# A fused attention and two-MLP kernel: weight conversion moved to the end of the first attention, and a second product in place of a copy

## The chip, the cores and the metric

One Trainium2 chip, one core of it. The metric is the device time of one execution in microseconds (us), median over the timed runs. The kernel before takes 1229.46 us (3 runs, 1223.87 to 1230.96).

## What is computed

Three stages follow each other; tokens are rows.

```python
# attention: q, k, v of 4 batches x 12 heads x 448 positions x 64
scores = 30 * tanh(q @ k.T / sqrt(64) / 30)
attn   = exp(scores - max) / (sum + 1e-9)
x      = attn @ v                      # to 1792 tokens x 768
# MLP 1, d_ff 1536
x      = (sigmoid(x @ w_gate) * (x @ w_val)) @ w_out
# MLP 2, d_ff 2048
h      = x @ w_in
out    = (h * cos(h)) @ w_out2
```

The five weight matrices are float64 in memory (the reference draws them so); q, k, v are float32. The result is float32.

## The kernel before

**Halves.** The four batches go in two halves of two batches (896 tokens). The order is: attention of half 0, MLP 1 of half 0 (with the first steps of half 1's attention beside its last product), the rest of the attention of half 1, MLP 1 of half 1, then MLP 2 of half 1 and of half 0. Heads go in pairs, two heads side by side on the 128 partitions. A half has 12 pairs; below they are pair 0 to pair 11. Pairs 0 to 5 are the first batch of the half, 6 to 11 the second.

**Number format.** A product of float32 accuracy is made of three TensorE products: an operand is kept as a rounded high part and a low part (fp32r), and high x high, high x low, low x high are added (`mm3`, L510 to L523, six matmuls for each 128 rows of the contraction, two of each kind). So activations and weights are both "split": a copy that rounds, and a subtraction.

**Weights.** A weight unit is 128 x 768 numbers. It comes as pairs of 32-bit words and is made float32 by two ScalarE instructions (absolute value L158 and sign L160) and four VectorE ones (L165, L167, L171, L175: two with one input, two with two inputs in SBUF). It is stored to DRAM for the second half (`kept`, L248). Then it is split by ScalarE (L238, high part) and GpSimd (L239, low part, which reads the high part). In the program `w_front` is a unit's first part (absolute value, sign and the four), `w_back` the split; `w_step` does both, for different units. MLP 1 takes the units in the order gate 0, value 0, gate 1, value 1, and so on.

**Attention steps.** `attention` (L456) is a generator; a step `i` has four parts `c` = 0 to 3. In step `i`, pair `i` makes its scores (L393, tanh on ScalarE L396), pair `i-1` its exponentials' second half (L402), their sum (GpSimd L406, VectorE L410) and its product with v (`pv`, L422), pair `i-2` its normalisation: `den`, the sum over partitions on TensorE (L438), reciprocal (L441) and `r = pv * reciprocal` (L442) on VectorE, and in part 2 the split of the result `x` (`a_split`: the high part as a copy of `r` on VectorE, L450, the low part on GpSimd, L451). Pair `i+2` transposes q and k (`t`, L372) and splits them on VectorE (L376, L377). The transposes, `den` and `pv` share four PSUM banks. Steps 10 and 11 have no transposes left.

**Order.** Every engine runs its own instructions in the order in which the program records them; nothing is reordered. So where a weight piece is recorded between attention parts is where it runs, on each engine. `w_pieces` (L295) yields after every single piece of a unit: absolute value, sign, four VectorE pieces, split. `UNIT_PIECES` (L83) lists the places (i, c) at which one piece is recorded, `UNIT_LOADS` (L82) the places at which a unit's load is issued on SyncE's queue. Before, three units (gate 0, value 0, gate 1) are done in 21 pieces, in parts 1 and 3 of steps 2 to 11 and one in what is drained at the end (L504).

**From attention to MLP 1.** The last two attention parts are recorded inside `mlp1` (L547), behind the first four of six contraction steps of gate 0. So TensorE's order there is: `den` of pair 10, four steps of gate 0, `pv` of pair 11, `den` of pair 11, four steps of value 0, the last two steps of gate 0, the last two of value 0, then gate 1. After gate 0's end ScalarE makes the sigmoid (L553, behind a table load), and the `w_step` behind it records value 1's first part and then the split of one unit.

Of the kernel before, what the change touches and what calls it, by code (L numbers as in the profile page):

```python
# [11 lines left out]
ALU = mybir.AluOpType  # L12
# [15 lines left out]
def softcap_attention_gated_mlp_cos_mlp(  # L28
# [18 lines left out]
    nc = tc.nc  # L47
    B, H, S, D = q.shape
# [4 lines left out]
    NP = H // 2  # L53
    KD, KF, KF2 = DM // P, DFF // P, DFF2 // P
    BH = 2
# [23 lines left out]
    PVS = ((), (), (0, 1, 2, 3), ())  # L79
    NORM, SPLIT = 0, 2  # L80

    UNIT_LOADS = ((1, 1), (3, 1), (6, 1))  # L82
    UNIT_PIECES = [(i, c) for i in range(2, BH * NP) for c in (1, 3)]  # L83

    WARM = {(0, 0, 0): 2, (0, 0, 1): 1}

# [179 lines left out]
    def w_early():  # L266

        for _ in w_signs():
            pass

    def w_front(mid=nothing):

        if pos["conv"] == len(units):
            mid()
            return
        if pos["sign"] == pos["conv"]:
            w_early()
        for i, _ in enumerate(w_conv()):
            if i == 1:
                mid()  # L280
        w_loads()
# [13 lines left out]
    def w_pieces(n):  # L295

        for _ in range(n):
            if pos["keep"] < pos["conv"]:
                w_keep()
            yield from w_sign()  # L300
            yield
            yield from w_conv()
            yield
            if pos["keep"] == pos["split"]:
                w_keep()
            w_split()
            yield
# [28 lines left out]
    zeros = tmp.tile([P, S], F32, tag="tmp", name="zeros")  # L336
    pairs = [(b, hp) for b in range(B) for hp in range(NP)]

    pieces = w_pieces(len(UNIT_LOADS))
    raw_q, v_t, st_t, p_t, s_t, pv_t, r_t = {}, {}, {}, {}, {}, {}, {}  # L340
    x_t = {}

# [91 lines left out]
    def a_norm(b, hp):  # L434
        s = s_t.pop((b, hp))
        den = psA.tile([P, 512], F32, tag="A", name=f"den{b}_{hp}")
        for h in range(2):
            nc.tensor.matmul(den[h * D : (h + 1) * D, :S], lhsT=ones[:CP], rhs=s[:CP, h, :], start=True, stop=True)  # L438
        pv = pv_t.pop((b, hp))
        r = tmp.tile([P, 2, S], F32, tag="tmp", name=f"r{b}_{hp}")  # L440
        nc.vector.reciprocal(out=r[:, 0], in_=den[:, :S])  # L441
        nc.vector.tensor_tensor(out=r[:, 1], in0=pv[:, :S], in1=r[:, 0], op=ALU.mult)  # L442
        r_t[b, hp] = r

    def a_split(b, hp, engine):
        r = r_t.pop((b, hp))
        if b % BH == 0:
            x_t[hp] = big_tile([P, 2, BH, S], F32R, f"x{b}_{hp}")
        x = x_t[hp]
        nc.vector.tensor_copy(out=x[:, 0, b % BH], in_=r[:, 1])  # L450
        engine.tensor_tensor(  # L451
            out=x[:, 1, b % BH], in0=r[:, 1], in1=x[:, 0, b % BH].bitcast(F32), op=ALU.subtract
        )

    def attention(hf):


        lo, hi = hf * BH * NP, (hf + 1) * BH * NP
        mine = pairs[lo:hi]
        n = len(mine)  # L460
        a_load(*mine[0])
        a_load(*mine[1])
        a_load(*mine[2])
        a_load_v(*mine[0])
        yield
        a_prep(*mine[0], 0)
        a_prep(*mine[0], 1)
        yield
        a_prep(*mine[1], 0)
        a_prep(*mine[1], 1)  # L470
        yield
        for i in range(n + 1):
            if i + 3 < n:
                a_load(*mine[i + 3])
            for c in range(NC):
                if i + 1 < n and c == 3:
                    a_load_v(*mine[i + 1])
                if i < n:
                    a_scores(*mine[i], c)
                if i and c == 0:  # L480
                    a_exp(*mine[i - 1], 1)
                if i < n and c == 2:
                    a_exp(*mine[i], 0)
                if i and c == 2:
                    a_sum(*mine[i - 1])
                if i + 2 < n and c % 2 == 0:
                    a_prep(*mine[i + 2], c // 2)
                if 1 < i < n and c == NORM:
                    a_norm(*mine[i - 2])
                if i:  # L490
                    for cc in PVS[c]:
                        a_pv(*mine[i - 1], cc)
                if 1 < i < n and c == SPLIT:
                    a_split(*mine[i - 2], nc.gpsimd)
                if i >= n - 1 and c == 3:
                    a_norm(*mine[i - 1])
                if i == n and c == 0:
                    a_split(*mine[i - 2], nc.gpsimd)
                if hf == 0 and (i, c) in UNIT_LOADS:
                    w_load()  # L500
                if hf == 0 and (i, c) in UNIT_PIECES:
                    next(pieces, None)
                yield
        if hf == 0:  # L504
            for _ in pieces:
                pass
        a_split(*mine[n - 1], nc.vector)


# [21 lines left out]
    def mlp1(hf, before, beside):  # L531
# [3 lines left out]
        x = [x_t[i] for i in range(KD)]  # L535
        g = []
        for m in range(KF):
            ps = {}
            for part in ("g", "v"):
                w = w_take()  # L540
                ps[part] = ps_tile(f"p{part}{hf}_{m}")
                if m == 0:
                    for kk in range(KD - 2):
                        mm3(ps[part], w, kk, x[kk], kk == 0, False)
                    if part == "g":
                        w_first = w
                        for _ in before:  # L547
                            pass
                        continue
                    for kk in (KD - 2, KD - 1):  # L550
                        mm3(ps["g"], w_first, kk, x[kk], False, kk == KD - 1)
# [22 lines left out]
        for m in range(KD):  # L574
            ps = ps_tile(f"py{hf}_{m}")
            for s in range(2):
                w = w_take()
                for kk in range(KF // 2):
                    i = s * KF // 2 + kk
# [203 lines left out]
```

## Time and profile before

| what | value |
|---|---|
| timed runs, median of 3 | 1229.46 us (1223.87 to 1230.96) |
| the profiled execution's own time | 1220.99 us |
| its span | 1219.2 us |
| granted TensorE clock, mean | 0.998 |
| PE (TensorE) busy | 1195.7 us, 98% |
| DVE (VectorE) busy | 687.5 us, 56% |
| ACT (ScalarE) busy | 592.3 us, 49% |
| POOL (GpSimd) busy | 445.6 us, 37% |

All durations below come from that one profiled execution, so a sum over them stands against 1220.99 us. It lies below the shortest timed run. In the page's 40 equal slices of the span TensorE is busy for 90% or more in all but four (the first, the third, one near 745 us and the last). The first attention lies in the first 130 us, the second one mostly from 390 to 490 us. TensorE's granted clock is 1.00 in the stretches used below.

### The profile page before, as it was taken

The page shows a single profiled execution, that of the slowest core. Times are in us where ns is not written, and L with a number is a line of the kernel's source. Part 1 is how long each engine was busy: PE and PEld are TensorE (multiplying, and loading weights), DVE is VectorE, ACT ScalarE, POOL GpSimd, SP SyncE. Part 2 cuts the span into 40 slices and gives each one's busy share as a digit, 9 for nine tenths or more (in the row PEclk, how much of TensorE's full clock was granted, in tenths as well). Part 3 has the DMA queues.
Part 4 walks back from the last instruction along what each step waited for, and adds up shares of the span by engine and source line. Part 5 has one row for each costly group of instructions (what it writes and reads, how often), then busy time and mean ns, then how long its engine had stood idle before and what let it go on. Part 6 is the DMA issues. An engine that isn't in the chain of part 4 may idle for free.

```text
span 1219.2 us, 15898 instructions
## 1 busy us (share of the span) xinstructions
PE 1195.7 (98%) x6347; PEld 1033.7 (85%) x6347; DVE 687.5 (56%) x729; ACT 592.3 (49%) x664; POOL 445.6 (37%) x234
## 2 busy tenths in 40 slices
PE   8989999999999999999999998999999999999998
PEld 4444889999987555999999997899999999999998
DVE  6998688778732997556566574511514534024242
ACT  6886455444425885444444345533506345344250
POOL 2767123223314665223233222522514333335140
PEclk9999999999999999999999999999999999999999
DMA  6431565555833340275655674121211631213003
GB/s 157 124 99 49 163 219 166 168 168 169 231 131 104 86 135 4 90 225 177 220 169 188 212 231 160 55 65 43 64 59 33 200 104 46 72 33 100 18 27 98
DMA packets 127083, 148.17 MB, mean 122 GB/s; under 512 B 50081, under 2 KB 100641, under 8 KB 127009
## 3 DMA queue, kind: packets, MB, share of 16 engines
q1 hardware_dynamic: 126720, 147.09, 39.1%
q8 instruction: 50, 0.82, 0.3%
q14 instruction: 25, 0.20, 0.0%
q10 hardware_dynamic: 288, 0.07, 0.0%
HBM read 112.13 MB, written 35.00 MB: 121 GB/s over the span
## 4 chain that ended last, share of the span: by engine, by line
PE 75%; DVE 13%; ACT 4%; DMA 4%; issue 2%; SPq 1%; POOL 0%; DVEq 0%; ACTq 0%; POOLq 0%
PE po L638 17%; PE ph L517 16%; PE pg L517 13%; PE pv L517 12%; PE py L517 7%; PE pv L422 4%; PE s L393 3%; DVE r L441 2%; DMA wz_raw<-in_moe_w_out_dram 2%; PE more L638 1%; PE t L372 1%; DVE f L171 1%; PE den L438 1%; DMA wi_raw<-in_moe_w_in_dram 1%; DVE fb L171 1%
## 5 line engine op out<-in xcount | busy, mean ns | idle before, releaser
L239 POOL TENSOR_TENSOR w<-f,w 128x768 fp32r<-128x768 f32 (+1 forms) x140 | 269.5, 1931 | 662.4 <-ACT w L238 572.8
L638 PE MATMUL po<-w,z 128*128 128x384 f32 x1248 | 221.0, 335 | 1.9 <-POOL w L239 1.9
L638 PEld LDWEIGHTS po<-w,z 128*128 128x128 f32 x1248 | 216.8, 188 | 2.9 <-POOL w L239 2.8
L517 PE MATMUL pv<-x,w 128*128 128x448 f32 x864 | 180.0, 366 | 0.9 <-DVE sg L566 0.9
L517 PE MATMUL pg<-x,w 128*128 128x448 f32 x864 | 179.9, 366 | 0.0
L517 PE MATMUL py<-g,w 128*128 128x448 f32 x864 | 177.5, 366 | 0.0
L517 PEld LDWEIGHTS pv<-x,w 128*128 128x128 f32 x864 | 162.0, 188 | 15.9 <-issue 3.0
L517 PEld LDWEIGHTS pg<-x,w 128*128 128x128 f32 x864 | 162.0, 188 | 14.7 <-ACT p L396 0.7
L517 PEld LDWEIGHTS py<-g,w 128*128 128x128 f32 x864 | 161.7, 188 | 13.5 <-issue 1.0
L685 DVE TENSOR_SCALAR n<-u 128x896 f32<-128x896 f32 (+1 forms) x38 | 29.4, 773 | 181.6 <-ACT u L684 181.6
L238 ACT CAST w<-f 128x768 fp32r<-128x768 f32 (+1 forms) x140 | 112.2, 809 | 39.3 <-DVE f L175 16.2
L517 PE MATMUL ph<-y,w 128*128 128x448 f32 (+1 forms) x578 | 119.9, 369 | 3.3 <-ACT y L590 2.8
L517 PEld LDWEIGHTS ph<-y,w 128*128 128x128 f32 x578 | 109.3, 190 | 13.3 <-ACT y L590 3.2
L517 PE MATMUL ph<-ya,w 128*128 128x448 f32 (+2 forms) x579 | 118.2, 365 | 0.0
L517 PEld LDWEIGHTS ph<-ya,w 128*128 128x128 f32 x579 | 108.4, 188 | 9.1
L396 ACT ACTIVATE p<-s,tanh_scale 112x896 f32<-112x896 f32 x96 | 93.0, 1011 | 43.0 <-PE s L393 42.9
L402 ACT ACTIVATE p<-p,cap_sb 112x1792 f32<-112x1792 f32 x48 | 86.3, 1798 | 0.1
L393 PEld LDWEIGHTS s<-st 64*112 64x112 f32 x576 | 45.7, 171 | 40.9 <-ACT p L396 19.0
L422 PE MATMUL pv<-p,v 112*64 112x448 f32 x384 | 77.5, 545 | 2.7 <-PE t L372 2.7
L441 DVE RECIPROCAL r<-den 128x448 f32<-128x448 f32 x24 | 70.8, 2950 | 8.7 <-PE den L438 8.7
L393 PE MATMUL s<-st 64*112 64x448 f32 x576 | 73.3, 380 | 1.5 <-ACT p L396 1.4
L406 POOL TENSOR_TENSOR sum<-p 112x896 f32<-112x896 f32 x24 | 55.9, 2330 | 49.1 <-ACT p L402 24.1
(82 smaller groups left out, 1201.8 us busy)
## 6 DMA issues: line engine op xcount, KB each, us to landing
f<-kept SPq DMA_DIRECT2D x96, 384.0 KB, 3.1
kept<-f SPq DMA_DIRECT2D x36, 384.0 KB, 2.7
wi_raw<-in_moe_w_in_dram SPq DMA_DIRECT2D x16, 768.0 KB, 5.8
kept<-fb SPq DMA_DIRECT2D x30, 384.0 KB, 2.7
wz_raw<-in_moe_w_out_dram SPq DMA_DIRECT2D x14, 768.0 KB, 5.2
wg_raw<-in_moe_w_gate_dram SPq DMA_DIRECT2D x12, 768.0 KB, 4.9
wv_raw<-in_moe_w_val_dram SPq DMA_DIRECT2D x12, 768.0 KB, 5.2
wo_raw<-in_moe_w_out_dram SPq DMA_DIRECT2D x12, 768.0 KB, 4.8
```

Source lines behind the costliest of these rows:

```text
L171: nc.vector.scalar_tensor_tensor(out=gi, in0=lo, scalar=28, in1=gi, op0=ALU.logical_shift_right, op1=ALU.bitwise_or)
L238: nc.scalar.copy(out=t[:, 0], in_=r)
L239: nc.gpsimd.tensor_tensor(out=t[:, 1], in0=r, in1=t[:, 0].bitcast(F32), op=ALU.subtract)
L393: nc.tensor.matmul(ps[:CP, h, :S], lhsT=st[r, ki, ks], rhs=st[r, qi], start=(n == 0), stop=(n == 2))
L396: nc.scalar.activation(out=pt[:CP, j], in_=ps[:CP, :, :S], func=AF.Tanh, scale=tanh_scale[:CP])
L402: nc.scalar.activation(out=pt[:CP], in_=pt[:CP], func=AF.Exp, scale=cap_sb[:CP])
L406: nc.gpsimd.tensor_tensor(out=s, in0=pt[:CP, 1] if half == 0 else s, in1=pt[:CP, 0], op=ALU.add)
L422: nc.tensor.matmul(pv[h * D : (h + 1) * D, :S], lhsT=tv[:, h, c, :], rhs=pt[:CP, j, h, :], start=(c == 0), stop=(c == NC - 1),)
L441: nc.vector.reciprocal(out=r[:, 0], in_=den[:, :S])
L517: nc.tensor.matmul(ps[:, c, s0:s1], lhsT=w[:, wi, kk, :], rhs=x[:, xi, c, s0:s1], start=(first and (wi, xi) == (0, 0)), stop=(last and (wi ...
L638: nc.tensor.matmul(pos_t[t][:, :NB], lhsT=zf[kk][:, zi, t * P : (t + 1) * P], rhs=ws[kk // UK][:, wi, kk % UK, :], start=(kk == 0 and (zi, ...
L685: nc.vector.tensor_scalar_add(out=n[:, c], in0=u[:, c], scalar1=ROUND)
```

## The change

Three edits. (1) `UNIT_LOADS` and `UNIT_PIECES` are rewritten: gate 0's pieces are spread over steps 2 to 10, value 0's lie in steps 10 to 12, and only two units are made in pieces (`FIRST`). (2) The third unit, gate 1, is converted by a `w_front` behind the last attention part, and so after the split of pair 11; its split is left to the `w_step` behind the sigmoid. (3) `a_split` makes the high part of x as a second product of `pv` and the reciprocal, from PSUM, where it copied `r`; so `pv` keeps its PSUM bank until then.

```diff
-    UNIT_LOADS = ((1, 1), (3, 1), (6, 1))
-    UNIT_PIECES = [(i, c) for i in range(2, BH * NP) for c in (1, 3)]
+    UNIT_LOADS = ((1, 1), (6, 1), (9, 1))
+    UNIT_PIECES = [(2, 1), (2, 2), (3, 3), (5, 3), (7, 3), (9, 3), (10, 1), (10, 2), (10, 3)]
+    UNIT_PIECES += [(11, 3), (11, 3), (12, 0), (12, 1), (12, 2)]
+    FIRST = 2
...
-    pieces = w_pieces(len(UNIT_LOADS))
+    pieces = w_pieces(FIRST)
...
-        pv = pv_t.pop((b, hp))
+        pv = pv_t[b, hp]
         r = tmp.tile([P, 2, S], F32, tag="tmp", name=f"r{b}_{hp}")
...
-        nc.vector.tensor_copy(out=x[:, 0, b % BH], in_=r[:, 1])
+        nc.vector.tensor_tensor(out=x[:, 0, b % BH], in0=pv_t.pop((b, hp))[:, :S], in1=r[:, 0], op=ALU.mult)
...
-                if hf == 0 and (i, c) in UNIT_PIECES:
+                for _ in range(UNIT_PIECES.count((i, c)) if hf == 0 else 0):
                     next(pieces, None)
...
                         for _ in before:
                             pass
+                        if hf == 0:
+                            w_front()
                         continue
```

The new lines shift what follows: L450 becomes L452, L175 becomes L177, L238 becomes L240.

In the rows of the order the first number of a name is the pair within its batch (`r_4` is pair 4 or 10) and the last number is the program's own count. VectorE, from the reciprocal of pair 10 to the split of pair 11, before:

```order
L441 RECIPROCAL r_4_1155<-den_4_1152 128x448
L442 TENSOR_TENSOR r_4_1155<-pv_4_1133,r_4_1155 128x448
L175 SCALAR_TENSOR_TENSOR f_989<-f_989,wg_raw 128x768
L450 CAST x_4_774<-r_4_1155 128x448
L410 SCALAR_TENSOR_TENSOR sum_5_1130<-sum_5_1130,guard,p_5_1_1120 112x896
L441 RECIPROCAL r_5_1201<-den_5_1198 128x448
L442 TENSOR_TENSOR r_5_1201<-pv_5_1189,r_5_1201 128x448
L450 CAST x_5_857<-r_5_1201 128x448
L451 TENSOR_TENSOR x_5_857<-r_5_1201,x_5_857 128x448
```

Four pieces of value 0 now stand ahead of the sum of pair 11, where one piece of gate 1 stood. The same place on VectorE, after:

```order
L443 RECIPROCAL r_4_1141<-den_4_1138 128x448
L444 TENSOR_TENSOR r_4_1141<-pv_4_1119,r_4_1141 128x448
L167 TENSOR_SCALAR f_1068<-f_1068 128x768
L169 TENSOR_SCALAR f_1068<-f_1068 128x768
L452 TENSOR_TENSOR x_4_763<-pv_4_1119,r_4_1141 128x448
L173 SCALAR_TENSOR_TENSOR f_1068<-wv_raw,f_1068 128x768
L177 SCALAR_TENSOR_TENSOR f_1068<-f_1068,wv_raw 128x768
L412 SCALAR_TENSOR_TENSOR sum_5_1116<-sum_5_1116,guard,p_5_1_1106 112x896
L443 RECIPROCAL r_5_1194<-den_5_1191 128x448
```

`f_1068` is value 0; gate 1's four pieces come behind the split of pair 11. ScalarE, from the last exponentials of pair 11 over the sigmoid (`sg_0`), before:

```order
L402 ACTIVATE p_5_1_1120<-p_5_1_1120,cap_sb 112x1792
L238 CAST w_1205<-f_989 128x768
L553 ACT_TABLE_LOAD
L553 ACTIVATE sg_0_1247<-pg_0_1163 128x896
L158 ACTIVATE f_1253<-wv_raw 128x768
L160 ACTIVATE wv_raw<-wv_raw,tiny 128x768
L238 CAST w_1263<-f_1253 128x768
L568 CAST g_0_1279<-sg_0_1247 128x896
```

Gate 1's split (`w_1205`) stands ahead of the sigmoid. The same place on ScalarE, after:

```order
L404 ACTIVATE p_5_1_1106<-p_5_1_1106,cap_sb 112x1792
L240 CAST w_1188<-f_1068 128x768
L160 ACTIVATE f_1201<-wg_raw 128x768
L162 ACTIVATE wg_raw<-wg_raw,tiny 128x768
L557 ACT_TABLE_LOAD
L557 ACTIVATE sg_0_1247<-pg_0_1152 128x896
L160 ACTIVATE f_1250<-wv_raw 128x768
L162 ACTIVATE wv_raw<-wv_raw,tiny 128x768
L240 CAST w_1259<-f_1201 128x768
L572 CAST g_0_1275<-sg_0_1247 128x896
```

Value 0's split is now there, and gate 1's (`w_1259`) stands behind the sigmoid and behind value 1's absolute value and sign. ScalarE in steps 10 and 11, after (before, none of the three weight rows stood between the scores of these two pairs):

```order
L398 ACTIVATE p_4_0_1015<-s_4_1_1032,tanh_scale 112x896
L240 CAST w_1041<-f_403 128x768
L398 ACTIVATE p_4_1_1044<-s_4_2_1045,tanh_scale 112x896
L404 ACTIVATE p_4_0_1015<-p_4_0_1015,cap_sb 112x1792
L160 ACTIVATE f_1068<-wv_raw 128x768
L398 ACTIVATE p_4_1_1044<-s_4_3_1072,tanh_scale 112x896
L162 ACTIVATE wv_raw<-wv_raw,tiny 128x768
L398 ACTIVATE p_5_0_1081<-s_5_0_1082,tanh_scale 112x896
L404 ACTIVATE p_4_1_1044<-p_4_1_1044,cap_sb 112x1792
```

Three weight instructions now stand ahead of pair 10's second half of exponentials.

## Rows read from the trace of the kernel before

**Rows 1.** Chain of waits, start and end of VectorE's stretch: start us, us, what
```profile
23.77 0.64 DVE st L376
...
85.68 1.07 DVE sum L410
```

**Rows 2.** Busy time of each engine in four stretches: stretch, its us, engines
```profile
24.00:90.00 66.00, 59.38 (x386) 30.14 (x384) 65.24 (x67) 57.39 (x51) 43.02 (x24) 1.00 0.41 112
404.00:452.00 48.00, 48.00 (x320) 24.31 (x318) 47.38 (x49) 42.77 (x37) 33.29 (x19) 1.00 0.37 97
457.00:472.00 15.00, 14.73 (x95) 6.21 (x91) 12.09 (x11) 14.92 (x14) 11.25 (x7) 1.00 0.03 9
130.00:204.00 74.00, 73.12 (x358) 66.91 (x358) 64.23 (x62) 40.59 (x47) 22.79 (x11) 1.00 0.61 192
```

**Rows 3.** Timeline of TensorE, first attention: start us, us, line, operation [idle before]
```profile
23.66 0.97 PE L438 MATMUL den<-sum,ones 112*64 112x448 f32 x4
...
94.56 0.97 PE L438 MATMUL den<-sum,ones 112*64 112x448 f32 x4 [0.30 <-DVE sum L410]
...
109.75 0.97 PE L438 MATMUL den<-sum,ones 112*64 112x448 f32 x4 [1.44 <-DVE sum L410]
...
118.85 0.92 PE L438 MATMUL den<-sum,ones 112*64 112x448 f32 x4
...
129.75 7.57 PE L517 MATMUL pg<-x,w 128*128 128x448 f32 x36
```

**Rows 4.** Waits of TensorE from 130 to 212 us: us in total, times, longest
```profile
PE pv L517 <- DVE sg L566: 0.9, 2, 0.5
```

**Rows 5.** Timeline of TensorE, the same places of the second attention
```profile
394.66 0.97 PE L438 MATMUL den<-sum,ones 112*64 112x448 f32 x4
...
457.55 0.97 PE L438 MATMUL den<-sum,ones 112*64 112x448 f32 x4
...
471.06 0.97 PE L438 MATMUL den<-sum,ones 112*64 112x448 f32 x4 [0.27 <-DVE sum L410]
...
490.76 7.46 PE L517 MATMUL pg<-x,w 128*128 128x448 f32 x36
```

**Rows 6.** By line, the two instructions on r: ns min/median/max
```profile
L450 DVE CAST x<-r x24: 379/1108/2185, 30.8 to 484.7; 128x448 fp32r<-128x448 f32 x24
...
L442 DVE TENSOR_TENSOR r<-pv,r x24: 624/624/626, 27.9 to 484.0; 128x448 f32<-128x448 f32 x24
```

**Rows 7.** Timeline, GpSimd's sum and the copy beside it, second attention
```profile
432.53 2.37 POOL L406 TENSOR_TENSOR sum<-p 112x896 f32<-112x896 f32 x1 [1.35 <-issue]
...
434.04 1.12 DVE L450 CAST x<-r 128x448 fp32r<-128x448 f32 x1
```

**Rows 8.** Timeline of VectorE, weight pieces, one held up and two not
```profile
46.51 2.44 DVE L171 SCALAR_TENSOR_TENSOR f<-wg_raw,f 128x768 int32<-128x768 int32 x1
...
130.51 0.56 DVE L165 TENSOR_SCALAR f<-f 128x768 f32<-128x768 f32 x1 [5.99 <-ACT f L158]
...
131.70 0.96 DVE L171 SCALAR_TENSOR_TENSOR f<-wv_raw,f 128x768 int32<-128x768 int32 x1
```

**Rows 9.** Timeline of VectorE and GpSimd between the last two `den`
```profile
111.93 1.15 POOL L451 TENSOR_TENSOR x<-r,x 128x448 fp32r<-128x448 f32 x1
...
114.30 1.67 DVE L175 SCALAR_TENSOR_TENSOR f<-f,wg_raw 128x768 int32<-128x768 int32 x1
...
116.19 1.14 DVE L410 SCALAR_TENSOR_TENSOR sum<-sum,guard,p 112x896 f32<-112x896 f32 x1
```

**Rows 10.** Timeline of ScalarE and GpSimd behind the sigmoid
```profile
129.60 0.88 ACT L158 ACTIVATE f<-wv_raw 128x768 f32<-128x768 f32 x1
130.51 1.01 ACT L160 ACTIVATE wv_raw<-wv_raw,tiny 128x768 f32<-128x768 f32 x1
...
133.76 0.83 ACT L238 CAST w<-f 128x768 fp32r<-128x768 f32 x1 [2.23 <-DVE f L175]
...
134.67 1.85 POOL L239 TENSOR_TENSOR w<-f,w 128x768 fp32r<-128x768 f32 x1 [14.57 <-ACT w L238]
```

## The prediction

> **What bounds the kernel now.** Read the page's busy shares first: TensorE is at 98%, so only places where it idles, or works below its pace, can pay. The chain of waits shows one: from 23.77 to 86.7 us it runs on VectorE without leaving it [rows 1]. The busy times by stretch say the same: from 24 to 90 us VectorE works 65.24 of 66 us, TensorE 59.38 [rows 2]. The second attention is the same code without weight pieces, and in it TensorE is busy 48.00 of 48 us [rows 2]. So the second attention is the yardstick for the first. From the `den` of pair 0 to gate 1's first matmul the first takes 129.75 - 23.66 = 106.1 us [rows 3], the second 490.76 - 394.66 = 96.1 [rows 5]. Ten microseconds, 0.8% of the kernel, are all that a better order can win here, and 0.9 us more of waits that follow in MLP 1 [rows 4].
>
> In parts: pair 0 to pair 8 takes 70.9 us against 62.9, pair 8 to pair 10 15.2 against 13.5 [rows 3, 5]. Pair 10 to pair 11 takes 9.1 us and pair 11 to gate 1 10.9 [rows 3]. The change shortens the first part and lengthens the other three.
>
> **The copy that becomes a product.** The high part of x took 379 to 2185 ns as a copy, median 1108; the product `r`, with the same operands as the new one, took 624 to 626 ns in all 24 cases [rows 6]. The copy's long cases lie beside GpSimd: GpSimd's sum ran to 432.53 + 2.37 = 434.90, and the copy, begun at 434.04, ended 0.26 us behind it [rows 7]. The product is never held up. So a steady step loses about 1.1 - 0.6 = 0.5 us of VectorE, and the two instructions have no other user waiting but GpSimd's low part. The Trainium skill ("VectorE: DVE Perf Modes", section "The perf-mode tier table (the rule you actually need)") speaks against the edit: a float32 copy inside SBUF runs at twice the rate, a tensor_tensor or anything with a PSUM operand at one. By the rule alone the product would cost 0.625 - 0.379 = 0.25 us more each; the trace bears it out only for the shortest copies, and the median decides for me.
>
> In the second attention a step of VectorE is about 48/6 = 8.0 us, TensorE's the same or a little less: 62.9/8 = 7.9 [rows 2, 5]. VectorE falls to 7.5 there and TensorE stays the bound. That half gains nothing.
>
> **Steady steps of the first attention, pair 0 to pair 8.** One unit leaves them whole, and the other's four VectorE pieces go to steps 3, 5, 7 and 9: two of 0.56 and two of 0.96 us, 3.0 in all [rows 8]. Steps are 7.5 us of VectorE against 7.9 of TensorE, so a piece of 0.6 to 1.0 us, with some 0.6 us behind GpSimd's sum, makes VectorE late by about 1 us and the next steps win 0.4 each back. TensorE feels it only at `den`. There a new wait comes: since `pv` keeps its bank longer, `den` now gets the bank of the last transposes of k, and waits for their second row on VectorE as well as for the sum. What is queued behind that `den` are the next scores, and behind them tanh. I put 0.6 us on TensorE for the pieces and for the sign on ScalarE in step 2. Bounds: 0, if all is hidden, as in the second attention; 5.8, if all 3.0 us and four waits of 0.7 (a piece held up took 2.44 in place of 0.96, at most twice that [rows 8]) land on the path. So 62.9 + 0.6 = 63.5 us.
>
> **Steps 10 and 11, pair 8 to pair 10.** Here ScalarE is the bound: 14.92 of 15 us in the second attention [rows 2], and its `den` of pair 10 waits for the sum, thus for pair 10's exponentials [rows 5]. The change puts gate 0's split, value 0's absolute value and its sign ahead of these. Each row begins some 0.1 us before the one ahead of it has ended, so they cost 0.73 + 0.78 + 0.91 = 2.4 us [rows 10]. Behind pair 10's `den` waits gate 0's first product, so it all lands on TensorE. 13.5 + 2.4 = 15.9 us. Bounds 13.5 and 16.3 (the durations in full, 2.7).
>
> **Pair 10 to pair 11.** In the kernel before, VectorE ended pair 11's sum at 116.19 + 1.14 = 117.3, 7.6 us after pair 10's `den` began, and TensorE had gate 0's four steps and `pv` to do until 118.85 [rows 3, 9]. Now this stretch loses one piece of gate 1 (1.67, 0.7 of it waiting [rows 9]) and a short copy (0.38), and gets value 0's four pieces (3.0), a product (0.62), and the waits behind GpSimd: 0.9 for pair 11's second sum and 1.15 for pair 10's low part, which comes free between the third and the fourth piece [rows 8, 9]. 7.6 - 2.05 + 3.6 + 2.05 = 11.2 us. So pair 11's `den` is late by 2.1 us, and TensorE has nothing else. Bounds: 9.1 (its own work) and 12.3 (one wait of 1.15 more). Value 0's split is ready at about the same time as the product that takes it.
>
> **Pair 11 to gate 1.** The third unit's four pieces run behind the split of pair 11 on an idle VectorE, hidden by TensorE's 10 us. Its split is late. Before, gate 1's first matmul came at 129.75, just behind the sigmoid [rows 3]. Now ScalarE first makes value 1's absolute value and sign, from 129.60 to 131.4, then gate 1's high part, to 132.2, and GpSimd the low part, 1.85 us, from 132.3 to 134.2 [rows 10]. The first four matmuls (0.8 us of 36 in 7.57 [rows 3]) need only the high part; the next need the low one. TensorE stands 134.2 - 0.8 - 129.75 = 3.6 us. 10.9 + 3.6 = 14.5. Bounds: 10.9, and 15.6 if VectorE's pieces for value 1 hold GpSimd up by one wait (1.15).
>
> **Behind it.** VectorE's 0.9 us of lateness in MLP 1 [rows 4] shrinks since TensorE comes later and VectorE does not: 0.4, between 0 and 0.9. The loads move later too, but value 1's is issued behind value 0's last piece and first used behind the sigmoid, over 10 us later, so I cost them at nothing.
>
> **Sum.** 63.5 + 15.9 + 11.2 + 14.5 + 0.4 = 105.5 us against 106.1 + 0.9 = 107.0: 1.5 us less. What the steady steps win, 7.4, the tail gives back but for this. On the profiled 1220.99 that is 1219.5; that execution is 8.5 us below the median of the runs shown, so on the median 1229.5 - 1.5 = 1228. The lower bounds sum to 96.4 (10.6 less), the upper ones, 68.7 + 16.3 + 12.3 + 15.6 + 0.9 = 113.8, to 6.8 more.
>
> **Rivals.**
> - *The tail hides its work.* Were pair 11's sum and gate 1's split in time, 2.1 + 3.6 us less: 7.2 faster, 1222. For it: in the kernel before the same waits were all covered. Against: the order of ScalarE leaves no room, the split stands behind three instructions of 2.6 us.
> - *The new wait at `den` keeps the step long.* If the pieces' full 5.8 us arrive, the steady part is 68.7: 3.7 slower than before, 1233. For it: before, pieces held up for 1.5 us did stop TensorE. Against: half of the pieces are gone from these steps.
> - *Slower: the weights stay one unit behind.* From gate 1 on each unit is split one `w_step` later against TensorE. If value 1 and gate 2 come late by the same 3.6 us too, 7.2 more: 5.7 slower; with value 2, 9.3 slower, 1239. It decides where a conversion and its split end later than TensorE's 7.6 us for a unit allow [rows 3]. Against: VectorE idles 74 - 64.2 = 9.8 us from 130 to 204 [rows 2], and TensorE's own stop of 3.6 us gives it time.
> - *The copy was not what waited.* If GpSimd's wait moves from the copy to the next instruction, a steady step is 8.0 + 0.25 = 8.25 us of VectorE, not 7.5, and 8 steps cost 0.3 more each: 2.5, so 1 us slower, 1230.5. This is where the tier table of the Trainium skill, named above, would lead alone. Against: what follows the copy reads PSUM, as the product does.
>
> **How the numbers follow.** About 0.5% (6 us) is what a measurement can tell from no change; the three runs shown are 7 us apart. Forecast 0.62, tail hidden 0.13, long steps 0.12, units behind 0.08, wait moved 0.05. Of the hidden tail about two thirds are faster by over 6 us, with a little from the forecast's own spread: 0.12. Slower by over 6 us are most of the units behind and a corner of the long steps: 0.08. Between, 0.80. The range takes the bounds nearly whole, for the runs' own spread: 1221 to 1234.
>
> **What would show it.** Right: TensorE's `den` every 7.9 to 8.0 us up to pair 8, at about 87 us; the high part of x at 0.62 us in all 24 cases; pair 10's `den` near 103, waiting for the sum; pair 11's near 114, waiting again; then a stop of some 3.6 us in front of and just inside gate 1's product, ended by the split on ScalarE and GpSimd; VectorE no longer the chain from 24 to 86. Wrong: a `den` that waits in the steady steps, a product of x over 0.7 us, gate 1 without a stop, or stops at value 1 and gate 2 as well.

## The result, and the profile after

The changed kernel takes 1234.12 us (median of 17 runs, 1227.23 to 1237.59), the kernel before 1225.16 us in runs beside it (17 runs). The ratio over these runs is 1.0062, 95% interval 1.0046 to 1.0078: 7.6 us slower (the two medians lie 9.0 us apart), more than the half per cent that counts here, and just past the predicted range (1228, 1221 to 1234). The range was laid on the 1229.46 us of three runs, which are among the seventeen; on 1225.16 its upper end would have been 1230, so the miss is larger than the tenth of a microsecond by which the range was passed.

The profiled execution of the changed kernel took 1235.90 us, that of before 1220.99. About half of these 14.9 us is no work of the change: behind the first attention, 36 matmuls took 7.46 us in the profile of before [rows 5] and 7.60 in this one, both at a granted clock of 1.00, and the executions of the other kernels below have one or the other, some of them first one and then the other. So only the first attention and gate 1 are compared here, by their own times.

The busy time of TensorE, its loads, VectorE, ScalarE and GpSimd by stretch in the changed kernel; the number ahead of the last two is the granted clock:

```profile
24.00:90.00 66.00, 60.57 (x388) 30.75 (x386) 64.27 (x62) 54.89 (x48) 40.22 (x23) 0.97 0.37 96
130.00:204.00 74.00, 71.31 (x330) 63.85 (x329) 61.09 (x58) 39.49 (x46) 23.24 (x11) 0.95 0.61 192
...
70.00:74.00 4.00, 4.00 (x23) 2.52 (x24) 3.97 (x4) 2.39 (x3) 2.35 (x2) 0.68 0.00 0
134.00:138.00 4.00, 3.73 (x9) 2.86 (x10) 3.78 (x3) 0.08 (x1) 2.03 (x1) 0.50 0.16 58
138.00:142.00 4.00, 4.00 (x14) 3.56 (x14) 3.04 (x4) 3.42 (x4) 0.47 (x1) 0.65 0.86 271
```

Before, both long stretches had a clock of 1.00 [rows 2]; now it is 0.97 and 0.95. VectorE still fills the first one: 64.27 us where it was to have room. The timeline of TensorE at the places of [rows 3]:

```profile
23.62 0.97 PE L440 MATMUL den<-sum,ones 112*64 112x448 f32 x4
...
50.19 0.97 PE L440 MATMUL den<-sum,ones 112*64 112x448 f32 x4 [1.65 <-DVE st L379]
...
68.69 1.37 PE L440 MATMUL den<-sum,ones 112*64 112x448 f32 x4 [2.40 <-DVE st L379]
...
93.98 0.97 PE L440 MATMUL den<-sum,ones 112*64 112x448 f32 x4
...
109.91 0.97 PE L440 MATMUL den<-sum,ones 112*64 112x448 f32 x4 [0.29 <-DVE sum L412]
...
120.68 0.97 PE L440 MATMUL den<-sum,ones 112*64 112x448 f32 x4 [1.58 <-DVE sum L412]
...
134.02 1.86 PE L519 MATMUL pg<-x,w 128*128 128x448 f32 x4 [2.44 <-ACT w L240]
136.13 8.96 PE L519 MATMUL pg<-x,w 128*128 128x448 f32 x32 [0.25 <-POOL w L241]
144.93 7.60 PE L519 MATMUL pv<-x,w 128*128 128x448 f32 x36
```

Pair 0 to pair 8 takes 93.98 - 23.62 = 70.4 us, hardly less than before (70.9), though one of the two units has left it. The waits of TensorE from 20 to 212 us name what stands there: L379, the low part of the split of k on VectorE. `den` now takes the PSUM bank that these transposes of k had.

```profile
PE den L440 <- DVE st L379: 4.5, 3, 2.4
PE den L440 <- DVE sum L412: 3.1, 3, 1.6
PE pg L519 <- ACT w L240: 2.4, 1, 2.4
...
PE pv L424 <- PE t L374: 0.8, 1, 0.8
```

Why that split is late, the timelines of VectorE and GpSimd show between 38 and 48 us:

```profile
39.38 0.61 DVE L452 TENSOR_TENSOR x<-pv,r 128x448 fp32r<-128x448 f32 x1
39.91 2.18 DVE L167 TENSOR_SCALAR f<-f 128x768 f32<-128x768 f32 x1
42.00 0.61 DVE L378 CAST st<-t 128x448 fp32r<-128x448 f32 x1
...
46.71 2.14 DVE L412 SCALAR_TENSOR_TENSOR sum<-sum,guard,p 112x896 f32<-112x896 f32 x1
...
38.45 2.11 POOL L408 TENSOR_TENSOR sum<-p 112x896 f32<-112x896 f32 x1 [1.37 <-ACT p L404]
40.51 1.15 POOL L453 TENSOR_TENSOR x<-r,x 128x448 fp32r<-128x448 f32 x1
...
45.79 2.11 POOL L408 TENSOR_TENSOR sum<-p 112x896 f32<-112x896 f32 x1 [1.37 <-issue]
```

The product takes 0.61 us, as forecast. But the piece behind it, 0.56 us by itself, starts at 39.91 beside GpSimd's sum and ends only at 42.09: GpSimd's sum lasts to 40.56, then GpSimd's next operation, the low part of x, runs to 41.66, and then the piece. That makes VectorE 1.6 us late, so in the next step its own sum (1.14 us when nothing holds it) begins at 46.71, 0.92 us behind GpSimd's, and is held to 2.14. The pattern comes again at 57.99 (piece 1.85), 64.47 (sum 2.88) and 76.49 (piece 2.98). Together the three pieces and two sums took 7.7 us more than unheld.

### The profile page after: what moved, and what is told of

It reads as the page before. It is cut to its first block, busy times and chain, and to the rows that moved or that the text cites. A ratio compares the mean times of both kernels' runs of the same rounds, so it can differ in the third digit from the quotient of the medians.

```text
span 1234.1 us, 15917 instructions
## 1 busy us (share of the span) xinstructions
PE 1208.1 (98%) x6347; PEld 1035.3 (84%) x6347; DVE 694.6 (56%) x729; ACT 592.5 (48%) x664; POOL 440.2 (36%) x234
## 4 chain that ended last, share of the span: by engine, by line
PE 72%; DVE 12%; ACT 6%; DMA 6%; issue 2%; POOL 1%; SPq 1%; DVEq 0%; ACTq 0%; POOLq 0%
PE po L642 17%; PE ph L519 15%; PE pv L519 12%; PE pg L519 11%; PE py L519 7%; PE pv L424 3%; PE s L395 3%; DMA wz_raw<-in_moe_w_out_dram 2%; ACT p L398 2%; DMA wi_raw<-in_moe_w_in_dram 1%; DVE fb L167 1%; DVE r L443 1%; DVE fb L173 1%; PE more L642 1%; DVE fb L177 1%
## 5 line engine op out<-in xcount | busy, mean ns | idle before, releaser
L519 PE MATMUL pg<-x,w 128*128 128x448 f32 x864 | 185.9, 372 | 2.7 <-ACT w L240 2.4
L519 PE MATMUL pv<-x,w 128*128 128x448 f32 x864 | 183.1, 368 | 0.7 <-POOL w L241 0.7
L519 PE MATMUL py<-g,w 128*128 128x448 f32 x864 | 180.1, 368 | 0.0
L240 ACT CAST w<-f 128x768 fp32r<-128x768 f32 (+1 forms) x140 | 112.1, 808 | 39.3 <-DVE f L177 15.8
L408 POOL TENSOR_TENSOR sum<-p 112x896 f32<-112x896 f32 x24 | 52.9, 2206 | 53.5 <-ACT p L404 24.1
```

The source lines that it names most:

```text
L240: nc.scalar.copy(out=t[:, 0], in_=r)
L408: nc.gpsimd.tensor_tensor(out=s, in0=pt[:CP, 1] if half == 0 else s, in1=pt[:CP, 0], op=ALU.add)
L519: nc.tensor.matmul(ps[:, c, s0:s1], lhsT=w[:, wi, kk, :], rhs=x[:, xi, c, s0:s1], start=(first and (wi, xi) == (0, 0)), stop=(last and (wi ...
```

## The experiments

Each row gives us in the profile of that kernel: from `den` of one pair to that of another, from pair 11 to gate 1's first matmul, their sum, how many us the granted clock was 0.5 between 20 and 145 us, and the ratio of the times to the kernel before. Before's first four are those of [rows 3].

| kernel | 0 to 8 | 8 to 10 | 10 to 11 | 11 to gate 1 | sum | at 0.5 | ratio, 95% interval |
|---|---|---|---|---|---|---|---|
| before | 70.9 | 15.2 | 9.1 | 10.9 | 106.1 | 0 | 1 |
| changed | 70.4 | 15.9 | 10.8 | 13.3 | 110.4 | 10.2 | 1.0062 (1.0046 to 1.0078) |
| product alone | 73.8 | 15.6 | 9.0 | 10.9 | 109.3 | 3.4 | 1.0042 (1.0022 to 1.0062) |
| plan alone | 67.6 | 15.9 | 10.6 | 13.4 | 107.5 | 3.4 | 1.0019 (0.9999 to 1.0039) |
| last part early | 69.8 | 17.1 | 10.6 | 12.1 | 109.5 | 6.8 | 1.0013 (0.9992 to 1.0033) |
| early places | 63.6 | 15.9 | 10.8 | 13.4 | 103.6 | 3.4 | 0.9987 (0.9965 to 1.0009) |
| filled stop | 70.0 | 15.9 | 10.8 | 13.4 | 110.1 | 3.4 | 1.0029 (1.0016 to 1.0043) |
| both repairs | 63.6 | 15.9 | 10.8 | 12.1 | 102.4 | 0 | 0.9968 (0.9947 to 0.9989) |
| early places, copy | 69.5 | 15.9 | 10.6 | 13.4 | 109.3 | 6.8 | 1.0037 (1.0021 to 1.0053) |
| low part on VectorE | 71.0 | 19.8 | 10.4 | 12.0 | 113.2 | 10.2 | 1.0053 (1.0027 to 1.0080) |
| spread | 68.2 | 14.3 | 9.0 | 12.0 | 103.6 | 3.4 | 0.9952 (0.9927 to 0.9977) |
| no pieces, product | 63.0 | 23.1 | 10.6 | 13.4 | 110.0 | 13.7 | one run |
| no pieces, copy | 64.9 | 21.4 | 10.3 | 13.3 | 110.0 | 17.1 | one run |
| spread with gaps | 63.9 | 14.7 | 9.0 | 12.1 | 99.6 | 0 | 0.9926 (0.9899 to 0.9953) |

**Product alone**: the kernel before, with only this edit.

```diff
-        pv = pv_t.pop((b, hp))
+        pv = pv_t[b, hp]
...
-        nc.vector.tensor_copy(out=x[:, 0, b % BH], in_=r[:, 1])
+        nc.vector.tensor_tensor(out=x[:, 0, b % BH], in0=pv_t.pop((b, hp))[:, :S], in1=r[:, 0], op=ALU.mult)
```

> The kernel before with the product in place of the copy, and nothing else. Theory A (in the changed kernel a weight piece recorded behind the split of x runs into GpSimd's sum and then its low part, 1.3 to 2 us each; the product itself is good): the copies' waits of about 0.7 us go, but half of the pieces stand behind the split here too and take up the same wait. From the first den to that of pair 8 it takes 68 to 71 us (70.9 before, 70.4 in the changed kernel), the total is within 0.3% of before. Theory B (what costs is that pv keeps its bank, so den waits for the split of k's transposes): den waits for that split in most steps, the part takes 73 us or more, and the kernel is 3 us or more slower than before.

The numbers are those of theory B: the steady part grew to 73.8 us, the ratio is 1.0042. The wait that theory B names came too: `den` stands 7.7 us for the split of k, where before it stood 4.1 for the sum. The product alone is a loss in the old plan. In its timeline VectorE's sum is held once, which never happened before the change (1.14 us each time in the first attention). A row of TensorE's waits, then the timelines of VectorE and GpSimd:

```profile
PE den L438 <- DVE st L377: 7.7, 5, 2.9
...
74.18 2.33 DVE L167 TENSOR_SCALAR f<-f 128x768 int32<-128x768 int32 x1
...
85.66 2.99 DVE L410 SCALAR_TENSOR_TENSOR sum<-sum,guard,p 112x896 f32<-112x896 f32 x1
...
84.95 2.74 POOL L406 TENSOR_TENSOR sum<-p 112x896 f32<-112x896 f32 x1 [1.73 <-issue]
```

**Plan alone**: the changed kernel with the copy; so `pv` gives its bank back as early as before.

```diff
-        pv = pv_t[b, hp]
+        pv = pv_t.pop((b, hp))
...
-        nc.vector.tensor_tensor(out=x[:, 0, b % BH], in0=pv_t.pop((b, hp))[:, :S], in1=r[:, 0], op=ALU.mult)
+        nc.vector.tensor_copy(out=x[:, 0, b % BH], in_=r[:, 1])
```

> The changed kernel with the copy back in place of the product: the new places of the pieces alone. Theory A: the copy waits for GpSimd's sum itself, so the piece behind it finds GpSimd idle and takes 0.56 to 0.96 us; a step without a piece is 8.0 us of VectorE. From the first den to that of pair 8 65 to 67 us, 3 to 5 us faster than the changed kernel in all, with the stop in front of gate 1 and the slow clock behind it as they are. Theory B: den waits for no split of k any more and the part takes 63.5 us, 7 us faster than the changed kernel.

67.6 us, 2.8 less than with the product, and a little over theory A's 65 to 67: in the late places the copy is the better one. Its four pieces took 0.55, 0.56, 0.95 and 0.95 us, unheld: where the first stood beside GpSimd's sum, the copy ahead of it did the waiting (1.10 us at 39.83). But VectorE's sum still slips, five times up to pair 8, and these five take 6.2 us more than unheld, so VectorE loses nearly as much as with the product (7.7). What differs is when `den` can start behind a late sum:

```profile
46.02 2.89 DVE L412 SCALAR_TENSOR_TENSOR sum<-sum,guard,p 112x896 f32<-112x896 f32 x1
...
48.97 0.97 PE L440 MATMUL den<-sum,ones 112*64 112x448 f32 x4 [1.11 <-DVE sum L412]
```

Here `den` starts 0.06 us behind the end of the sum. In the changed kernel each of the three `den` that wait for the split of k starts 1.34 us behind it (50.19, against 46.71 + 2.14 = 48.85), because VectorE makes that split after the sum. Without this delay, an estimate from these numbers, 1.5 of their 4.5 us of waits would be left. So the kept bank is a part of what the product costs here, beside the held pieces; no run has the copy and the kept bank together, which would separate the two.

**Last part early**: the third unit's split follows its conversion at once.

```diff
                         if hf == 0:
                             w_front()
+                            w_back()
```

> The changed kernel with gate 1's split recorded right behind its conversion, ahead of the sigmoid. Theory A (two causes: late pieces in the steps, and a stop in front of gate 1 of 2.4 us that TensorE's granted clock answers with one half for 6.8 us): the split ends some 11.5 us behind pair 11's den, the stop is at most 1 us, the clock stays at 1.00 there, and the kernel is 4.5 to 6 us faster than the changed one; the steps up to pair 8 stay at 70 us. Theory C (the late gate 1 makes the whole loss): 7.5 us faster, as fast as before.

Gate 1's first matmul now waits for the sigmoid, not for its weights, 12.1 us behind pair 11, and no half clock follows it. Two falls of the clock remain in the steps (3.4 us each). The second, from 104.1 us, is new: it stands behind stops of 1.2 and 0.9 us that the changed kernel has as well, without a fall, and it is in the 17.1 of the table. The ratio is 0.0049 below the changed kernel's, which is theory A's 6 us.

**Early places**: the first unit's VectorE pieces one product earlier.

```diff
-    UNIT_PIECES = [(2, 1), (2, 2), (3, 3), (5, 3), (7, 3), (9, 3), (10, 1), (10, 2), (10, 3)]
+    UNIT_PIECES = [(2, 1), (2, 2), (3, 1), (5, 1), (7, 1), (9, 1), (10, 1), (10, 2), (10, 3)]
```

> The changed kernel with the four VectorE pieces of gate 0 moved from part 3 to part 1 of the same steps: behind the product r and ahead of the sum, where GpSimd has just ended or is ending its own sum. Theory A: the pieces take 0.6 to 1.0 us, no den waits for the split of k, the clock does not fall near 68 us, the part up to pair 8 takes 64 to 65.5 us in place of 70.4, and the kernel is 5 to 6.5 us faster than the changed one. Theory B: the den of the steps with a piece still waits, and under 2 us are won. Theory C: nothing is won.

63.55 us, where 63.5 had been forecast for the change, and 0.0075 of the ratio back (9 us, more than theory A's 5 to 6.5). The piece now stands between the reciprocal's product and VectorE's sum. In steps 5, 7 and 9 GpSimd has just ended its own sum there, and the piece is unheld; in step 3 it took 1.09 us. In each of these steps the sum starts ahead of GpSimd's:

```profile
44.85 1.14 DVE L412 SCALAR_TENSOR_TENSOR sum<-sum,guard,p 112x896 f32<-112x896 f32 x1
...
52.59 0.55 DVE L169 TENSOR_SCALAR f<-f 128x768 int32<-128x768 int32 x1
...
45.73 2.24 POOL L408 TENSOR_TENSOR sum<-p 112x896 f32<-112x896 f32 x1 [1.36 <-issue]
```

**Filled stop**: ten products of the identity with itself ahead of gate 1, read by nobody.

```diff
+    FILL = 10
...
+                    if hf == 0 and m == 1 and part == "g":
+                        fill = psA.tile([P, 512], F32, tag="A", name="fill")
+                        for _ in range(FILL):
+                            nc.tensor.matmul(fill[:, :P], lhsT=ident, rhs=ident, start=True, stop=True)
```

> The changed kernel, and ahead of the second unit's gate matmuls ten products of the identity with itself (128 columns each) into a bank of their own that nobody reads; they stand where TensorE stopped for 2.4 us behind the first attention. Theory A (the half clock of 6.8 us behind that stop is bought by the stop, and the stop by the late weights): gate 1's first matmul still starts 13 to 14 us behind den11, since w0 of that unit comes no earlier, but no stretch of half clock lies behind it, the 32 matmuls of pv1 and gate 2 come some 3.4 us sooner relative to gate 1, and the time falls by 2 to 4 us to about 1231. Rival B (the clock falls for another reason than the stop): a stretch of half clock stays at 133 to 142 us, and the time stays within 1 us of the changed kernel's 1234 or rises by the fill's 2 us.

Each of the ten products stands in the trace as two instructions:

```profile
131.21 2.39 PE L566 MATMUL fill<-ident 128*128 128x128 f32 x20
133.85 1.08 PE L520 MATMUL pg<-x,w 128*128 128x448 f32 x4 [0.25 <-ACT w L241]
135.95 6.75 PE L520 MATMUL pg<-x,w 128*128 128x448 f32 x32 [1.02 <-POOL w L242]
142.54 7.96 PE L520 MATMUL pv<-x,w 128*128 128x448 f32 x36
...
134.00:138.00 4.00, 2.98 (x14) 2.44 (x15) 3.61 (x3) 0.26 (x1) 1.90 (x1) 1.00 0.23 81
```

The weights come no sooner, but the clock stays at 1.00: gate 1's first matmul to value 1's takes 142.54 - 133.85 = 8.7 us, against 10.9 in the changed kernel and 7.4 before. So the late low part costs 1.3 us, and the half clock behind the stop 2.2 (where it lasted 3.4 us in place of 6.8, as in "early places", 1.6); the ratio is 0.0033 lower, 4 us. Theory A held; its 3.4 us for the clock was too much, since TensorE waits through a part of the stretch.

**Both repairs**: the edits of "early places" and "last part early" in one.

> The changed kernel with two edits: the four pieces behind the second product of steps 3, 5, 7 and 9 stand behind the first of these steps (as in the run with that edit alone, 1224.8), and the third unit's last part follows its first in the first half of the second stage (as in the run with that edit alone, 1227.7). Theory A (two losses that add: pieces held beside GpSimd's sum and low part, and late weights with a stop and a half clock behind it): den8 63.5 us behind den0, den11 27 us behind that, gate 1 12.1 us behind den11, no half clock at gate 1, together 102.7 us against 106.1 before, so 1221 to 1223, ratio 0.996 to 0.998. Rival B (the two are one loss, moved about): gate 1's wait is 13 us again or the half clock comes back at another stop in these 110 us, and the time is 1224 to 1226.

In the profile the two losses add: 102.4 us, and no half clock in these stages. The ratio fell by 0.0094, where the two edits alone took 0.0075 and 0.0049, which their intervals allow. At 0.9968 it is faster than before, by 0.3%.

**Early places, copy**: "early places" with the copy of "plan alone".

> The changed kernel with the four pieces one product earlier (behind the first product of steps 3, 5, 7 and 9), and with the copy of before in place of x's second product. Theory A (the places of the pieces are the whole loss, and the product is worth little once they are clear of GpSimd's work): den8 64 to 66 us behind den0 and a time within 1.5 us of the run with these places and the product (1224.8). Rival B (the product is what the new places need: the copy, 1108 ns at the median beside GpSimd's sum, is held there as the pieces were): den8 67 us or later and a time 3 us or more above that run, 1228 or more.

Rival B came true: 69.5 us and 1232.31, 5.9 us more than with the product up to pair 8, and 0.0050 more of the ratio (6 us). In the early places the product is worth 6 us; in the late ones it cost 2.8. Neither edit has a price of its own.

**Low part on VectorE** (first attention only):

```diff
-                    a_split(*mine[i - 2], nc.gpsimd)
+                    a_split(*mine[i - 2], nc.vector if hf == 0 else nc.gpsimd)
```

> The changed kernel with x's low part (the subtraction behind the product, in the first attention) on VectorE instead of GpSimd; the pieces stay in their late places. Theory A (a piece in the late place waits for two of GpSimd's operations, the sum and the low part that is queued behind it): the pieces that took 1.85 to 2.98 us take 0.6 to 1.6 us, as they wait for the sum's end alone; the low part costs VectorE 0.6 to 1.0 us each step, partly in its idle time; den8 66 to 70 us behind den0. Rival B (the sum alone holds them): the pieces still take 1.8 us or more, den8 is 71 to 76 us and the time 2 to 5 us over the changed kernel's.

With no low part queued on GpSimd, three of the four pieces took 0.55, 0.55 and 0.94 us; the fourth (in step 9) 2.85. These are theory A's pieces, but with rival B's 71.0 us. They do not decide what held the pieces: behind the low part they start only some 0.4 us after GpSimd's sum has ended (41.65, against 38.75 + 2.49 = 41.24). That two operations of GpSimd held them is read from the changed kernel's own timeline above. The time did not fall: in these steps the low part is itself held once (1.77 us) and three sums are, and VectorE has 0.6 us more to do in each.

```profile
31.73 1.77 DVE L453 TENSOR_TENSOR x<-r,x 128x448 fp32r<-128x448 f32 x1
...
41.65 0.55 DVE L167 TENSOR_SCALAR f<-f 128x768 f32<-128x768 f32 x1
46.83 2.35 DVE L412 SCALAR_TENSOR_TENSOR sum<-sum,guard,p 112x896 f32<-112x896 f32 x1
...
38.75 2.49 POOL L408 TENSOR_TENSOR sum<-p 112x896 f32<-112x896 f32 x1 [1.30 <-ACT p L404]
```

**No pieces**: the first unit's four VectorE pieces and its split all in step 10, once with the product and once with the copy; what is read is the time to pair 8.

```diff
-    UNIT_PIECES = [(2, 1), (2, 2), (3, 3), (5, 3), (7, 3), (9, 3), (10, 1), (10, 2), (10, 3)]
+    UNIT_PIECES = [(2, 1), (2, 2)] + [(10, 1)] * 5 + [(10, 2), (10, 3)]
```

> The changed kernel with no VectorE piece in the steps 3 to 9 (the first unit's four pieces and its last part stand together in step 10); only the time to den8 is asked for. Theory A (the product by itself lets VectorE's sum start ahead of GpSimd's each time, so that nothing is held): steps of 7.93 us, den8 62.9 to 63.5 us behind den0, VectorE's sum 1.14 to 1.3 us in every step. Rival B (the product itself brings the steps out of time, pieces or not): steps of 8.5 us or more, den8 67 us or later.

> The same with the copy of before in place of x's second product. Theory A (the copy reads and writes SBUF, can be held beside GpSimd's sum, and then sends VectorE's sum behind GpSimd's next one): several steps of 8.5 us or more though no piece is there, den8 66 to 70 us. Rival B (a copy of 379 ns is shorter than a product of 615 and only pieces do harm): den8 62 to 64 us, no later than with the product.

With the product, every step up to pair 7 but one (8.05) is 7.93 us, pair 8 is reached at 63.0, and from pair 2 on VectorE's sum starts 1.2 to 1.3 us ahead of GpSimd's each time:

```profile
83.70 1.15 DVE L412 SCALAR_TENSOR_TENSOR sum<-sum,guard,p 112x896 f32<-112x896 f32 x1
...
85.02 2.12 POOL L408 TENSOR_TENSOR sum<-p 112x896 f32<-112x896 f32 x1 [1.36 <-issue]
```

With the copy the steps are 7.9 us at first too, but VectorE's sum comes every 7.98 us, GpSimd's every 7.93. VectorE's lead shrinks by some 0.05 us a step until it is lost, and then the step to pair 8 takes 9.3 us (7.4 with the product). The timelines of the copy's run, the last sum ahead of GpSimd's and the first behind it:

```profile
77.23 1.14 DVE L412 SCALAR_TENSOR_TENSOR sum<-sum,guard,p 112x896 f32<-112x896 f32 x1
85.22 3.04 DVE L412 SCALAR_TENSOR_TENSOR sum<-sum,guard,p 112x896 f32<-112x896 f32 x1
...
77.28 3.06 POOL L408 TENSOR_TENSOR sum<-p 112x896 f32<-112x896 f32 x1 [1.32 <-issue]
85.20 2.11 POOL L408 TENSOR_TENSOR sum<-p 112x896 f32<-112x896 f32 x1 [1.33 <-issue]
```

0.05 us ahead, VectorE takes 1.14 us and GpSimd is held; 0.02 us behind, it takes 3.04. The Trainium skill ("SBUF — State Buffer", section "Who interferes with whom") says so: a VectorE instruction with two inputs in SBUF contends with a GpSimd instruction that reads SBUF, the port pair they share is an exclusive lock, and "Issue order, not op shape, decides who blocks." The trace agrees with that: the one behind takes 0.95 us longer here in one order (3.06 in place of 2.11) and 1.9 in the other. Theory A was right on the mechanism and too high on the size (64.9 for 66 to 70): it expected several long steps, and one came.

**Spread**: "both repairs", with one piece in each of the steps 3 to 6 and 8 to 11.

```diff
-    UNIT_LOADS = ((1, 1), (6, 1), (9, 1))
+    UNIT_LOADS = ((1, 1), (4, 1), (9, 1))
...
+    UNIT_PIECES = [(2, 1), (2, 2), (3, 1), (4, 1), (5, 1), (6, 1), (7, 1), (7, 2), (7, 3)]
+    UNIT_PIECES += [(8, 1), (9, 1), (10, 1), (11, 1), (12, 2)]
```

> The version with both repairs (pieces behind the first product of a step, third unit's last part in the first half of the second stage; 1222.5 there) with the first two units spread evenly: one VectorE piece in each of the steps 3 to 6 and 8 to 11, the first unit's last part in step 6, the second load two steps sooner. Theory A (a piece that starts behind the first product costs a step some 0.3 us, since VectorE's work fills 7.8 of 7.93 us, while four of them in the last two steps cost 2 to 3 us): den8 64 to 65.5 us behind den0, den8 to den11 24 to 25.5 us against 26.7, gate 1 no later behind den11, 1220 to 1223. Rival B (where VectorE's sum slips behind GpSimd's once, the steps stay long): den8 67 us or later and 1225 or more; the first unit's last part on ScalarE and GpSimd in step 6 would be what tips it.

Both came in part: against "both repairs" 3.4 us are won in the last steps and 4.7 lost in the steady ones (the ratio is a little lower all the same, inside both intervals), where VectorE's sum is held twice. The first time it slips after two long pieces in neighbouring steps:

```profile
52.90 0.95 DVE L173 SCALAR_TENSOR_TENSOR f<-wg_raw,f 128x768 int32<-128x768 int32 x1
61.27 0.95 DVE L177 SCALAR_TENSOR_TENSOR f<-f,wg_raw 128x768 int32<-128x768 int32 x1
62.13 3.01 DVE L412 SCALAR_TENSOR_TENSOR sum<-sum,guard,p 112x896 f32<-112x896 f32 x1
...
61.98 2.22 POOL L408 TENSOR_TENSOR sum<-p 112x896 f32<-112x896 f32 x1 [1.36 <-issue]
...
71.25 1.83 POOL L241 TENSOR_TENSOR w<-f,w 128x768 fp32r<-128x768 f32 x1 [1.11 <-ACT w L240]
71.58 2.45 DVE L412 SCALAR_TENSOR_TENSOR sum<-sum,guard,p 112x896 f32<-112x896 f32 x1
```

The second time, at 71.58, it stands behind the low part of the first unit, begun on GpSimd at 71.25. That is the unit's last part, which rival B names (in the edit it lies in step 7). It comes behind the first slip, so it is not what tipped the steps.

**Spread with gaps**: an empty step before each long piece of the first unit, and that unit's last part one step later than in "spread".

```diff
-    UNIT_PIECES = [(2, 1), (2, 2), (3, 1), (4, 1), (5, 1), (6, 1), (7, 1), (7, 2), (7, 3)]
-    UNIT_PIECES += [(8, 1), (9, 1), (10, 1), (11, 1), (12, 2)]
+    UNIT_PIECES = [(2, 1), (2, 2), (3, 1), (4, 1), (6, 1), (8, 1), (8, 2), (8, 3), (9, 0)]
+    UNIT_PIECES += [(9, 1), (10, 1), (11, 1), (11, 3), (12, 2)]
```

> The spread version with its pieces set so that no two of the long ones (0.95 us) stand in neighbouring steps: the first unit's four in the steps 3, 4, 6 and 8 and its last part in step 8, the second unit's in 9, 10 and twice in 11. Theory A (VectorE has some 0.1 us to spare in a step, so that one piece makes its sum late and an empty step is needed before the next, or the sum starts behind GpSimd's and is held to 2.4 to 3.0 us): VectorE's sum 1.14 us in every step to 9, den8 63.4 to 64.5 us behind den0 instead of 68.2, den8 to den11 23 to 24.5 us, gate 1 some 12 us behind den11 and no half clock in the first attention; 1216 to 1220. Rival B (the two slips of the spread version came from the second unit's early load or from its first unit's last part in step 6, not from the pieces' sequence): den8 67 us or later, 1221 or more.

```profile
23.33 0.97 PE L440 MATMUL den<-sum,ones 112*64 112x448 f32 x4
...
87.25 0.97 PE L440 MATMUL den<-sum,ones 112*64 112x448 f32 x4
...
110.92 0.92 PE L440 MATMUL den<-sum,ones 112*64 112x448 f32 x4
...
122.97 7.56 PE L519 MATMUL pg<-x,w 128*128 128x448 f32 x36 [1.02 <-ACT sg L558]
```

No sum is held (1.13 to 1.18 us in each step), and the clock does not fall in these stages. The early load of the second unit is as in "spread", so rival B's one cause is out; its other, the last part, moved with the pieces and is not separated from them for the second slip. 1218.59 us (6 runs), ratio 0.9926 (0.9899 to 0.9953): faster than both kernels. The stages shown give 6.5 us of it; its interval is 5.8 to 12.4, and whether more is won behind gate 1 stays open.

## Why the prediction was wrong, step by step

**The steady steps failed.** The step that failed is "a piece of 0.6 to 1.0 us, with some 0.6 us behind GpSimd's sum, makes VectorE late by about 1 us and the next steps win 0.4 each back", hence "62.9 + 0.6 = 63.5 us". It measured 70.4, beyond even its upper bound of 68.7. Three things in it were wrong:
- *The wait of a piece.* A piece in the late place waited 1.3 to 2.0 us: for GpSimd's sum and for the low part behind it, which the product itself had just released. Even the upper bound gave each piece a wait of only 0.7, though the row cited for it shows one of 1.48 (2.44 in place of 0.96); with 1.48 it would have been 62.9 + 3.0 + 5.9 = 71.8, with 70.4 inside. The product took the copy's wait away and handed it to the instruction behind. The prediction dismissed this rival ("if GpSimd's wait moves from the copy to the next instruction", 0.05) because that instruction reads PSUM. In steps 3, 5, 7 and 9 it is a piece, which reads SBUF. "Plan alone" shows the other side: there the copy waits and the pieces are unheld.
- *The recovery.* Lateness is not won back bit by bit. As soon as VectorE's sum starts behind GpSimd's, it is held for another 1.0 to 1.9 us. "No pieces, copy" shows the edge within 0.07 us, "spread with gaps" that an empty step between long pieces keeps the lead.
- *The bank.* The prediction named the wait of `den` for the split of k and put 0.6 us on all that TensorE feels. Behind a late sum it makes `den` 1.3 us later still, about 3 of the 4.5 us of these waits by the estimate under "plan alone". Where the sum is ahead of GpSimd's, the kept bank costs next to nothing: two waits of 0.2 us in "early places".

TensorE met this where the prediction looked for it, at `den`, by the split of k: the 0.12 rival "keeps the step long" had place and sign right, with too small a size. Of the 7.5 us over 62.9, 4.5 are these waits, 0.8 a wait of `pv` for its transposes, and 1.5 the 3.4 us at half clock behind the stop of 2.40 us: with no other wait listed in it, the step from that `den` to the next takes 78.13 - 68.69 = 9.44 us in place of 7.93. The other 0.7 is spread in smaller pieces.

```profile
78.13 0.97 PE L440 MATMUL den<-sum,ones 112*64 112x448 f32 x4
```

**The product's own time** was right: 24 of them, median 615 ns, 611 to 618, none held. To price it alone was wrong.

**Steps 10 and 11**: 15.9 forecast, 15.9 measured, and by the mechanism forecast: ScalarE is busy for 16.00 of the 16 us from 94 to 110. **Pair 10 to 11**: 11.2 forecast, 10.8 measured, waiting for the sum as described. **Gate 1**: a stop of 3.6 us was forecast; 2.4 us in front and 1.3 inside came, 3.7 together, ended by ScalarE and GpSimd as described. "Last part early" shows that its place is the cause. **Behind it**, 0.4 of waits were forecast and none is listed up to 212 us; so the rival by which value 1 and gate 2 come late too did not come.

**The clock was left out.** The sum has no term for what a stop does to the next matmuls; at gate 1 that is 2.2 us ("filled stop"), in the steps 1.5.

So: the forecast of -1.5, plus 6.9 from the steady steps, plus 2.2 from the clock at gate 1, less 0.8 for the two terms that came out low (pair 10 to 11 and the later waits), plus 0.1 at gate 1, is +6.9 us; the ratio says 7.6 (5.6 to 9.6).

## What to carry to other kernels

Where two engines can hold each other up, as VectorE and GpSimd do here, and meet once in every step, ask which of them starts first and by how much, before adding up durations: the same product in place of the copy was worth +2.8 or -5.9 us by the place of four small instructions. An instruction freed from a wait can pass that wait to the one behind it, so look at what that one reads. A buffer that is kept longer changes what its next user waits for. A stop of TensorE is to be priced with the granted clock of the matmuls behind it, as a cost that comes in some executions and not in others.

## What the hardware showed unexpectedly

- At the end of a GpSimd instruction, GpSimd's next queued one ran before the VectorE instruction that was waiting: all three pieces held in the steps up to pair 8 (39.91, 57.99, 76.49 us) ended behind both.
- Stops of 2.4 us were followed by granted clock 0.5 (1.2 GHz) for 3.4 us in some profiles and 6.8 us in others at the same place (gate 1: 6.8 in the changed kernel, 3.4 in "plan alone" and "early places"); stops of 1.0 to 1.2 us at gate 1 by none. In the steps a stop's length alone did not tell: one of 2.56 us in "product alone" (51.24) was followed by no fall, one of 1.57 in "early places, copy" (76.36) by one.
- 36 matmuls at clock 1.00 took 7.46 us in some executions and 7.60 in others, some 1.9% apart, whichever kernel it was; in "early places" 7.46 up to about 600 us and 7.60 behind it.
